# Attention followed by two MLPs: in five of the 24 head pairs both heads' values run on column halves, and the order of all instructions is planned anew

## The chip, the cores and the metric

The kernel runs on one core of one Trainium2 chip. Its engines are TensorE (PE in the profile, its weight loads PEld), VectorE (DVE), ScalarE (ACT), GpSimd (POOL) and SyncE (SP, which issues nearly all DMAs). The metric is the device time of one execution in microseconds (us); the lower, the better.

## The reference, cut to what matters

Three stages follow each other: an attention over 4 batches of 12 heads with 448 rows of 64, a first MLP with a softmax and a layer norm, and a second MLP with `h - tanh(h)`. All data are float32.

```python
def _attn_ref(q, k, v, g_q, g_k):
    q_n, k_n = (rmsnorm(q, g_q), rmsnorm(k, g_k))
    scores = scale * np.matmul(q_n, k_n.transpose(0, 1, 3, 2))
    scores = scores - np.max(scores, axis=-1, keepdims=True)
    attn = np.exp(scores)
    attn = attn / (np.sum(attn, axis=-1, keepdims=True) + 1e-09)
    return np.matmul(attn, v)
def _moe_ref(x, w_in, w_out, g_ln):
    h = x @ w_in
    e = np.exp(h - np.max(h, axis=-1, keepdims=True))
    solu = h * (e / (np.sum(e, axis=-1, keepdims=True) + 1e-09))
    ...
    return (ln @ w_out)
def _moe2_ref(x, w_in, w_out):
    h = x @ w_in
    return ((h - np.tanh(h)) @ w_out)
```

## The kernel before

The 48 heads are worked on as 24 pairs. For a pair, `qk_trans` transposes the normalised q and k (tile `qkps`), `maxima` forms the score rows to find their maxima (products `mps`, then a reduction `nm` on VectorE), `spread` brings the negated maxima into the operand of the next product (`nmps`, `nt`, and a DMA into `q`), and `weights` forms the transposed scores (`sps`) and their exponentials (`pf`, on ScalarE). `pv` multiplies them by the values. Its stationary operand is a tile `va` in which the 64 value columns of a chunk stand beside 64 columns of ones, so that one product gives 64 rows of sums weighted by the values and 64 rows of plain sums. It is a float32 product, and the profile has two records for each. A head has three chunks of 128 keys and a tail of 64; the tails of both heads lie on the two row halves of one tile, and `pv_tails` issues them one behind the other. So a pair has six full products and two tails, in two PSUM tiles `pvps`. `pv_fin` copies both halves of each out of PSUM on ScalarE (`sx`, `xu`), and `x_norm` divides and stores the result by a DMA (`xd`).

The first MLP runs in four blocks of tokens between the steps of the attention: its products are `hps` and `x2ps`, its transposes `lps`. Its weights are converted during the first blocks (tiles `raw`, `val`, `w`), saved to DRAM and loaded back later (`w<-w_in`, `w<-w_out`). The second MLP (`h2ps`, `ops`) follows when the attention is done.

Nothing of the order on the engines up to the end of the attention is the program's own: a `Recorder` takes each instruction down, and `place` plans a time for each from a table of costs. On each engine it takes the one with the lowest number in program order plus its entry in the table `SHIFT`. It adds margins for signals between engines (`slack`, two values: attention and MLP) and for DMAs (`doubt`), in us. Where the plan leaves TensorE without work, `fill` puts in products of a constant tile that nothing reads (tile `idle`, here called fillers). They stand in the program like any other product and run whether the wait for which they were planned comes or not.

```python
        took = 0.216 * (2 if since < self.warm else 1)
        n = int((start - since - 0.1) / took)
```

Since the recorder issues all instructions, they all carry the line L204.

Of the kernel before, what the change touches and what calls it, by code (L numbers as in the profile page):

```python
# [167 lines left out]
def _real(x):  # L168
# [3 lines left out]
SHIFT = {  # L172
    "bs vector": 61, "e scalar": 372, "gam scalar": 54, "gln scalar": -176, "glr load": -133, "grow load": 127,
    "hb scalar": 709, "hb vector": 727, "hps tensor": -61, "k scalar": 33, "k vector": -511, "lnT scalar": -27,
    "lnT vector": -468, "mv vector": -324, "nm vector": -5, "nmps tensor": -112, "nr scalar": 647, "nr vector": -428,
    "nt scalar": -1395, "ones vector": -357, "pf scalar": -1312, "pvps tensor": 76, "q gpsimd": -80, "q scalar": -59,
    "q sync": 43, "q vector": -148, "qd scalar": -121, "qd vector": 197, "qk load": 123, "qkps tensor": -1541,
    "qn gpsimd": -22, "qn vector": 18, "raw load": 176, "rr scalar": 128, "rr vector": 326, "rs gpsimd": 177,
    "rs vector": 7, "sm vector": 63, "sps tensor": 3, "sq scalar": 1359, "ss vector": 194, "sx scalar": -14,
    "va load": 108, "val scalar": 231, "val vector": -44, "w gpsimd": 21, "w scalar": -36, "w sync": 77,  # L180
    "w vector": -244, "w_in_ sync": -91, "w_out_ sync": 19, "wk scalar": 565, "wk vector": 5, "wq scalar": 1978,
    "x scalar": 22, "x2ps tensor": 312, "xd sync": 40, "xo scalar": 69, "xo vector": -253, "xr sync": -60,
    "xs scalar": 16, "xs vector": -126, "xu scalar": 232, "xu vector": 7, "zero vector": -3,
}


class Recorder:
# [14 lines left out]
    def take(self, eng, what, f, a, kw):  # L202
# [6 lines left out]
        outs = list(a[:1]) + [kw[n] for n in ("out", "accum_out") if n in kw]  # L209
        ins = list(a[1:]) + [x for n, x in kw.items() if n not in ("out", "accum_out")]  # L210
        op.out = outs[0]
# [25 lines left out]
        self.ops.append(op)  # L237

    def cost(self, op):
        n = 1  # L240
# [9 lines left out]
        if op.queue == "tensor":  # L250
            if op.what == "transpose":
                return (0.095 if n < 128 else 0.108), 0.2
            rhs = op.kw["rhs"]
            if rhs.root.dtype != F32:
                return 0.0025 + n * 0.000451, 0.2
            return (0.58 if rhs.p1 - rhs.p0 == 64 else 0.75), 0.2
# [48 lines left out]
    def transfer(self, op):  # L305
# [5 lines left out]
        return max(1, packets / 16.0) * (8 + 0.05 * run) * 1e-3  # L311

    def plan(self):
        for op in self.ops:
            op.after = 0.0
        for _ in range(self.passes):
            order = self.place()
            for op in self.ops:
                if op.eng == "dma" and not any(isinstance(x, View) for x in op.ins):
                    op.after = op.first - self.ahead  # L320
        return order

    def place(self):
# [36 lines left out]
        free = dict.fromkeys(("tensor", "vector", "scalar", "gpsimd", "sync"), 0.0)  # L360
        wire, lanes = 0.0, []
        ready = {e: [] for e in free}
        for op in ops:
# [29 lines left out]
        while placed < total:  # L393
# [28 lines left out]
            if e == "tensor" and start < self.warm:  # L422
                took *= 2
            if e == "vector" and op.what in ("tensor_tensor", "scalar_tensor_tensor", "tensor_scalar"):
                if took > 0.3 and not any(r.psum for r in op.refs) and start < free["gpsimd"]:
                    took += min(free["gpsimd"] - start, 1.1)
            if op.eng == "dma":
# [55 lines left out]
    warm = 9.0  # L483
    passes, ahead = 2, 185.2
    overlap = {"vector": 0.08, "scalar": 0.08, "gpsimd": 0.05}
    slack, doubt = (0.07, 0.18), 0.44
    still = None
# [11 lines left out]
def kernel(  # L499
# [180 lines left out]
    qk_t, qn_t, w_t, v_t, nm_t = {}, {}, {}, {}, {}  # L680
    pc_t, pv_t, xu_t, rb_t = {}, {}, {}, {}
    A = {}
    Q, K, qd = [], [], []

    def pair(p):
        return p // HP, 2 * (p % HP)
# [19 lines left out]
    def load_v(p):  # L706

        b, h = pair(p)
        t = v_t[p] = A["vh"].tile([128, 14, D], F32, tag="va", name="va")
        tv = t.rearrange("p (a z) d -> p a z d", z=2)  # L710
        nc.gpsimd.memset(tv[:, :, 1], 1.0)
        for i in range(2):
# [3 lines left out]
            )  # L716
        nc.sync.dma_start(out=tv[:, 6, 0], in_=v[b, h:h + 2, 384:448, :])

    def rsqrt(y, x, scale):
# [190 lines left out]
    def x_norm(p):  # L910
# [10 lines left out]
        nc.sync.dma_start(out=xd[:, hp, S * b:S * b + S], in_=xo)  # L921

    attn = []

    LAG = 7
# [4 lines left out]
    def step(i, *a):  # L930
        at(i // 4, i % 4, *a)

    for p in range(NP):
# [9 lines left out]
        for i in range(2):  # L943
            n, z = s + i, 4 * (s + i)
            for j, c in enumerate((3, 0, 1, 2) if i == 0 else (4, 5, 6)):
                step(z + j, maxima, p, c)
            step(z + 4, spread, n)
            for j in range(3):
                step(z + LAG + j, weights, n, j)
                step(z + LAG + 4 + j, pv, n, j)  # L950
        step(z + LAG + 3, weights, s + 1, 3)
        step(z + LAG + 4, pv_tails, s)
        step(z + LAG + 4, pv_fin, s)
        step(z + LAG + 6, pv_fin, s + 1)
        step(z + LAG + 8, x_norm, p)
    order = {maxima: 0, spread: 1, weights: 2, pv_tails: 3, pv: 4, pv_fin: 5}
    attn.sort(key=lambda e: (e[0], e[1], order.get(e[3], 6), e[2]))
# [421 lines left out]
```

## Time and profile before

| | us |
|---|---|
| median of 3 runs | 1060.19 |
| lowest and highest | 1055.9, 1064.42 |
| the profiled execution, its own time | 1062.6 |
| its span | 1060.8 |

The profiled execution has 1.8 us around its span and lies 2.4 us above the median. TensorE is busy through 98% of the span, and the attention ends at about 460 us. A time in the views counts from the start of the span.

### The profile page before, as it was taken

Reading aid. Unit: us, or ns where it says so; the run is one execution under the profiler, and the core shown is the slowest. Engines: PE = TensorE matmul, PEld = TensorE weight load, DVE = VectorE, ACT = ScalarE, POOL = GpSimd, SP = SyncE. Lnnn points to the kernel's source line nnn. Section 1 sums busy time; section 2 is a strip of 40 time slices with the busy share of each in tenths; the row PEclk is TensorE's granted clock in tenths of the full one; section 3 lists DMA queues with packets and bytes.
Section 4 is the critical chain, followed back from the end, with each engine's and each line's share of the span. In section 5 each row is a group of like instructions: output and inputs, shape, how many; then the busy total and the mean of one; then the engine's idle time right before and its main releaser. Section 6 shows DMA issues by size and latency. Waiting matters only on the chain.

```text
span 1060.8 us, 15538 instructions
## 1 busy us (share of the span) xinstructions
PE 1039.4 (98%) x5526; PEld 883.0 (83%) x5526; DVE 694.0 (65%) x1312; ACT 492.9 (46%) x996; POOL 235.1 (22%) x204
## 2 busy tenths in 40 slices
PE   8999999999999998999999999999999999999998
PEld 7666687677867887688999999898989999998987
DVE  8887877999898434557641373666767575765434
ACT  5888867888886544752451453212222221212110
POOL 3332223121122000025000251313333241422000
PEclk9999999999999998999999999999999999999999
DMA  7998999989999976387765421222212021110004
GB/s 188 212 255 239 245 259 275 256 219 303 300 311 332 266 205 188 112 274 249 253 229 189 164 62 59 60 61 60 60 40 78 22 61 43 57 60 1 1 30 179
DMA packets 112469, 171.20 MB, mean 161 GB/s; under 512 B 30656, under 2 KB 78216, under 8 KB 112392
## 3 DMA queue, kind: packets, MB, share of 16 engines
q1 hardware_dynamic: 112368, 170.20, 55.3%
q8 instruction: 44, 0.72, 0.3%
q14 instruction: 33, 0.27, 0.1%
q10 hardware_dynamic: 24, 0.01, 0.0%
HBM read 109.32 MB, written 29.10 MB: 130 GB/s over the span
## 4 chain that ended last, share of the span: by engine, by line
PE 87%; DMA 5%; DVE 4%; ACT 3%; issue 1%; SPq 0%; ACTq 0%; DVEq 0%
PE ops L204 22%; PE h2ps L204 22%; PE pvps L204 10%; PE hps L204 10%; PE x2ps L204 10%; PE sps L204 6%; PE mps L204 3%; PE qkps L204 2%; DMA raw<-in_moe_w_in_dram 1%; PE idle L204 1%; PE lps L204 1%; DVE nm L204 1%; ACT pf L204 1%; DMA w<-w_in 1%; DMA q<-nt 1%
## 5 line engine op out<-in xcount | busy, mean ns | idle before, releaser
L204 PE MATMUL ops<-w,gT 128*128 128x384 f32 x1344 | 257.5, 336 | 0.0
L204 PE MATMUL h2ps<-x2s,w 128*128 128x512 f32 (+1 forms) x1152 | 256.4, 365 | 0.0
L204 PEld LDWEIGHTS ops<-w,gT 128*128 128x128 f32 x1344 | 235.8, 188 | 8.4
L204 PEld LDWEIGHTS h2ps<-x2s,w 128*128 128x128 f32 x1152 | 200.2, 188 | 27.8
L204 DVE SCALAR_TENSOR_TENSOR val<-raw,val 128x512 int32<-128x512 int32 (+1 forms) x192 | 146.9, 767 | 63.4 <-POOL val L204 61.1
L204 DVE TENSOR_TENSOR ob<-ops,ob 128x384 f32<-128x384 f32 x196 | 108.3, 553 | 102.4 <-PE ops L204 102.0
L204 POOL TENSOR_TENSOR w<-val,w 128x512 fp32r<-128x512 f32 x60 | 80.7, 1347 | 380.5 <-ACT w L204 380.5
L204 PE MATMUL pvps<-pf,va 128*128 128x448 f32 (+1 forms) x384 | 158.5, 555 | 0.0
L204 PE MATMUL hps<-w,xs 128*128 128x256 f32 (+1 forms) x828 | 133.6, 315 | 3.2 <-DMA w<-w_in 3.2
L204 DVE TENSOR_REDUCE nm<-mps 128x1 f32<-128x448 f32 x168 | 101.0, 617 | 54.2 <-PE mps L204 53.3
L204 PE MATMUL sps<-q,k 128*128 128x448 f32 (+2 forms) x400 | 130.0, 430 | 6.1 <-ACT pf L204 3.1
L204 PEld LDWEIGHTS hps<-w,xs 128*128 128x128 f32 x828 | 118.8, 195 | 15.8 <-issue 3.5
L204 PE MATMUL x2ps<-lnT,w 128*128 128x384 f32 (+1 forms) x720 | 125.1, 328 | 0.3 <-DVE lnT L204 0.3
L204 PEld LDWEIGHTS x2ps<-lnT,w 128*128 128x128 f32 x720 | 118.2, 189 | 3.0 <-issue 1.5
L204 ACT ACTIVATE th<-h2ps 128x512 f32<-128x512 f32 (+1 forms) x64 | 34.8, 544 | 179.9 <-PE h2ps L204 161.9
L204 PEld LDWEIGHTS sps<-q,k 128*128 128x128 f32 (+2 forms) x400 | 68.9, 182 | 44.3 <-issue 18.6
L204 ACT ACTIVATE pf<-sps 128x448 f32<-128x448 f32 (+1 forms) x169 | 87.9, 537 | 31.0 <-PE sps L204 28.7
L204 PEld LDWEIGHTS pvps<-pf,va 128*128 128x128 f32 (+1 forms) x384 | 61.1, 188 | 37.5 <-issue 33.9
L204 POOL TENSOR_SCALAR val<-raw 128x512 f32<-128x512 f32 x48 | 80.1, 1670 | 25.1 <-DMA raw<-in_moe_w_out_dram 11.9
L204 ACT ACTIVATE gT<-th 128x512 fp32r<-128x512 f32 (+1 forms) x64 | 37.1, 579 | 98.6 <-PE ops L204 66.8
L204 POOL TENSOR_TENSOR qn<-qk,rr 112x512 f32<-112x512 f32 x44 | 50.2, 1159 | 118.2 <-DVE rr L204 60.8
L204 DVE TENSOR_TENSOR th<-h2ps,th 128x512 f32<-128x512 f32 (+1 forms) x64 | 39.7, 621 | 44.2 <-ACT th L204 44.1
(95 smaller groups left out, 992.1 us busy)
## 6 DMA issues: line engine op xcount, KB each, us to landing
w<-w_out SPq DMA_DIRECT2D x48, 512.0 KB
raw<-in_moe_w_in_dram SPq DMA_DIRECT2D x36, 512.0 KB
raw<-in_moe_w_out_dram SPq DMA_DIRECT2D x36, 512.0 KB
w<-w_in SPq DMA_DIRECT2D x24, 512.0 KB
q<-wq SPq DMA_DIRECT2D x46, 224.0 KB
k<-wk SPq DMA_DIRECT2D x46, 224.0 KB
w_in<-w SPq DMA_DIRECT2D x12, 512.0 KB
w_out<-w SPq DMA_DIRECT2D x12, 512.0 KB
```

Source lines behind the costliest of these rows:

```text
L204: return f(*[_real(x) for x in a], **{n: _real(x) for n, x in kw.items()})
```

## The change

For pairs 16 to 20 (`halves = range(16, 21)`) the products with the values are written differently. `load_v2` loads the values alone, without columns of ones and without GpSimd's memset. `pv2` issues for each chunk the products of both heads one behind the other: each has 64 columns, head 0 writes partitions 0 to 63 of one PSUM tile and head 1 partitions 64 to 127. `sums` adds the four exponential tiles of a head on GpSimd (three adds a head, of which the tails have 64 partitions), and `pv_sums` multiplies both heads' added tiles by 64 columns of ones on the two halves (`sups`). `x_norm2` works straight from the two PSUM tiles instead of `pv_fin`'s copies: two ScalarE instructions and three on VectorE a pair, where before there were six and three. The planner counts such a pair of products as one instruction of 0.76 us.

In the program this takes 40 products `pvps` of 128 columns away, and brings 40 of 64 columns and 10 `sups`; 30 adds come to GpSimd and 5 memsets go; 20 ScalarE instructions go. Of the rest only one kind of instruction has another count: the fillers are 162 instead of 88.

The planner has another rule for VectorE and GpSimd instructions that use SBUF at the same time, other margins (`slack`, `doubt`, `ahead`), and another `SHIFT`.

```diff
@@ -170,17 +170,19 @@
 SHIFT = {
-    "bs vector": 61, "e scalar": 372, "gam scalar": 54, "gln scalar": -176, "glr load": -133, "grow load": 127,
...
+    "bs vector": 1852, "e scalar": -388, "gam scalar": 178, "gln scalar": -555, "glr load": 501, "gps tensor": 103,
...
 }
@@ -207,7 +209,9 @@
         op.queue, op.what, op.f, op.a, op.kw = eng, what, f, a, kw
         op.at, op.rank = len(self.ops), self.rank
         outs = list(a[:1]) + [kw[n] for n in ("out", "accum_out") if n in kw]
-        ins = list(a[1:]) + [x for n, x in kw.items() if n not in ("out", "accum_out")]
+        ins = list(a[1:]) + [x for n, x in kw.items() if n not in ("out", "accum_out", "ins")]
+        for one in kw.get("ins", ()):
+            ins += [one["lhsT"], one["rhs"]]
         op.out = outs[0]
         name = op.out.root.args[3].rstrip("0123456789") if isinstance(op.out, View) else "-"
         load = op.eng == "dma" and not any(isinstance(x, View) for x in a[1:] + tuple(kw[n] for n in kw if n != "out"))
@@ -236,6 +240,14 @@
                 root.log = keep
         self.ops.append(op)
 
+    def both(self, two):
+        def f(**kw):
+            for one in two:
+                self.tensor.real.matmul(**{n: _real(x) for n, x in one.items()})
+
+        a, b = two
+        self.take("tensor", "both", f, (), dict(out=a["out"], accum_out=b["out"], ins=[a, b]))
+
     def cost(self, op):
         n = 1
         for d in (op.out.shape if isinstance(op.out, View) else [1, 1])[1:]:
@@ -250,6 +262,8 @@
         if op.queue == "tensor":
             if op.what == "transpose":
                 return (0.095 if n < 128 else 0.108), 0.2
+            if op.what == "both":
+                return 0.76, 0.2
             rhs = op.kw["rhs"]
             if rhs.root.dtype != F32:
                 return 0.0025 + n * 0.000451, 0.2
@@ -309,6 +323,13 @@
         if run < 64:
             return 0.025 * packets
         return max(1, packets / 16.0) * (8 + 0.05 * run) * 1e-3
+
+    @staticmethod
+    def shares(op):
+        if op.queue == "gpsimd":
+            return op.what != "memset"
+        two = op.what in ("tensor_tensor", "scalar_tensor_tensor", "tensor_scalar")
+        return op.queue == "vector" and two and not any(r.psum for r in op.refs)
 
     def plan(self):
         for op in self.ops:
@@ -359,6 +380,7 @@
         opened = dict.fromkeys(queue, 0)
         free = dict.fromkeys(("tensor", "vector", "scalar", "gpsimd", "sync"), 0.0)
         wire, lanes = 0.0, []
+        lock = {"vector": 0.0, "gpsimd": 0.0}
         ready = {e: [] for e in free}
         for op in ops:
             if op.left == 0:
@@ -421,9 +443,10 @@
             took, late = self.cost(op)
             if e == "tensor" and start < self.warm:
                 took *= 2
-            if e == "vector" and op.what in ("tensor_tensor", "scalar_tensor_tensor", "tensor_scalar"):
-                if took > 0.3 and not any(r.psum for r in op.refs) and start < free["gpsimd"]:
-                    took += min(free["gpsimd"] - start, 1.1)
+            if op.eng != "dma" and self.shares(op):
+                other = lock["gpsimd" if e == "vector" else "vector"]
+                took += max(other - start, 0.0)
+                lock[e] = start + took
             if op.eng == "dma":
                 if len(lanes) >= 8:
                     start = max(start, lanes[-8])
@@ -481,9 +504,9 @@
     notice = {"tensor": 0.02, "gpsimd": 0.045}
     lag = 0
     warm = 9.0
-    passes, ahead = 2, 185.2
+    passes, ahead = 2, 202.6
     overlap = {"vector": 0.08, "scalar": 0.08, "gpsimd": 0.05}
-    slack, doubt = (0.07, 0.18), 0.44
+    slack, doubt = (0.12, 0.39), 0.94
     still = None
 
     def give(self):
@@ -678,7 +701,8 @@
 
 
     qk_t, qn_t, w_t, v_t, nm_t = {}, {}, {}, {}, {}
-    pc_t, pv_t, xu_t, rb_t = {}, {}, {}, {}
+    pc_t, pv_t, xu_t, rb_t, su_t = {}, {}, {}, {}, {}
+    halves = range(16, 21)
     A = {}
     Q, K, qd = [], [], []
 
@@ -704,6 +728,10 @@
 
 
     def load_v(p):
+
+        if p in halves:
+            load_v2(p)
+            return
 
         b, h = pair(p)
         t = v_t[p] = A["vh"].tile([128, 14, D], F32, tag="va", name="va")
@@ -715,6 +743,16 @@
                 in_=v[b, h + i, 0:384, :].rearrange("(c p) d -> p c d", p=128),
             )
         nc.sync.dma_start(out=tv[:, 6, 0], in_=v[b, h:h + 2, 384:448, :])
+
+    def load_v2(p):
+
+        b, h = pair(p)
+        t = v_t[p] = A["vh"].tile([128, 14, D], F32, tag="va", name="va")
+        for i in range(2):
+            nc.sync.dma_start(
+                out=t[:, 3 * i:3 * i + 3], in_=v[b, h + i, 0:384, :].rearrange("(c p) d -> p c d", p=128)
+            )
+        nc.sync.dma_start(out=t[:, 6], in_=v[b, h:h + 2, 384:448, :])
 
     def rsqrt(y, x, scale):
 
@@ -920,6 +958,57 @@
         nc.vector.scalar_tensor_tensor(out=xo, in0=sx, scalar=-2.0, in1=xu, op0=ALU.add, op1=ALU.mult)
         nc.sync.dma_start(out=xd[:, hp, S * b:S * b + S], in_=xo)
 
+    def pv2(p, j):
+
+        if j == 0:
+            pv_t[p, 2] = ps_v.tile([128, 4, CP], F32, tag="v", name="pvps")
+        ps = pv_t[p, 2]
+        two = []
+        for i in range(2):
+            r = slice(64 * i, 64 * i + 64)
+            k = r if j == 3 else slice(0, 128)
+            two.append(dict(
+                out=ps[r], lhsT=v_t[p][k, 6 if j == 3 else 3 * i + j], rhs=pc_t[2 * p + i, j][k],
+                start=j == 0, stop=j == 3,
+            ))
+        nc.both(two)
+
+    def sums(n, j):
+
+        p, i = divmod(n, 2)
+        if i == 0 and j == 1:
+            rb_t[p] = A["one"].tile([128, S], F32, tag="sx", name="sx")
+            xu_t[p] = A["xu"].tile([128, S], F32, tag="xu", name="xu")
+        r = slice(64 * i, 64 * i + 64) if j == 3 else slice(0, 128)
+        o = (rb_t, xu_t)[i][p][r]
+        x, y = (pc_t[n, jj][r].rearrange("r c q -> r (c q)") for jj in (0, j))
+        nc.gpsimd.tensor_tensor(out=o, in0=x if j == 1 else o, in1=y, op=ALU.add)
+
+    def pv_sums(p):
+
+        ps = su_t[p] = ps_m.tile([128, 4, CP], F32, tag="m", name="sups")
+        nc.both([
+            dict(
+                out=ps[64 * i:64 * i + 64].rearrange("r c q -> r (c q)"), lhsT=nc.still[:, 0:64],
+                rhs=(rb_t, xu_t)[i][p], start=True, stop=True,
+            )
+            for i in range(2)
+        ])
+
+    def x_norm2(p):
+        b, hp = divmod(p, HP)
+        su, xu = (t.rearrange("r c p -> r p c") for t in (su_t.pop(p), pv_t.pop((p, 2))))
+        xo = A["xo"].tile([128, S], F32, tag="xo", name="xo")
+        y, t = rb_t.pop(p), xu_t.pop(p)
+        xo4, y4, t4 = (z.rearrange("r (p c) -> r p c", c=4) for z in (xo, y, t))
+
+        nc.scalar.activation(out=y4, in_=su, func=AF.Ln, bias=tiny)
+        nc.scalar.activation(out=y, in_=y, func=AF.Exp, scale=-1.0)
+        nc.vector.scalar_tensor_tensor(out=t4, in0=su, scalar=tiny, in1=y4, op0=ALU.add, op1=ALU.mult)
+        nc.vector.scalar_tensor_tensor(out=xo4, in0=xu, scalar=-1.0, in1=y4, op0=ALU.mult, op1=ALU.mult)
+        nc.vector.scalar_tensor_tensor(out=xo, in0=t, scalar=-2.0, in1=xo, op0=ALU.add, op1=ALU.mult)
+        nc.sync.dma_start(out=xd[:, hp, S * b:S * b + S], in_=xo)
+
     attn = []
 
     LAG = 7
@@ -945,15 +1034,30 @@
             for j, c in enumerate((3, 0, 1, 2) if i == 0 else (4, 5, 6)):
                 step(z + j, maxima, p, c)
             step(z + 4, spread, n)
+            if p in halves:
+                for j in range(3):
+                    step(4 * s + LAG + 2 * j + i, weights, n, j)
+                    if j:
+                        step(4 * s + LAG + 2 * j + i + 1, sums, n, j)
+                for j in (0, 1) if i == 0 else (2, 3):
+                    step(4 * s + LAG + 2 * j + 2, pv2, p, j)
+                continue
             for j in range(3):
                 step(z + LAG + j, weights, n, j)
                 step(z + LAG + 4 + j, pv, n, j)
+        if p in halves:
+            step(4 * s + LAG + 6, weights, s + 1, 3)
+            step(4 * s + LAG + 7, sums, s, 3)
+            step(4 * s + LAG + 7, sums, s + 1, 3)
+            step(4 * s + LAG + 9, pv_sums, p)
+            step(4 * s + LAG + 10, x_norm2, p)
+            continue
         step(z + LAG + 3, weights, s + 1, 3)
         step(z + LAG + 4, pv_tails, s)
         step(z + LAG + 4, pv_fin, s)
         step(z + LAG + 6, pv_fin, s + 1)
         step(z + LAG + 8, x_norm, p)
-    order = {maxima: 0, spread: 1, weights: 2, pv_tails: 3, pv: 4, pv_fin: 5}
+    order = {maxima: 0, spread: 1, weights: 2, pv_tails: 3, pv: 4, pv_fin: 5, sums: 3, pv_sums: 4, pv2: 5}
     attn.sort(key=lambda e: (e[0], e[1], order.get(e[3], 6), e[2]))
     attn_i = [0]
 
```

The first place is TensorE at the products with the values of pair 16. `mps` and `nmps` are of the next pair, `sps` the scores of pair 17. Before:

```order
L204 MATMUL pvps<-pf,va 128x448 x2
L204 MATMUL mps<-k_178,q_161 128x448
L204 MATMUL pvps<-pf,va 128x448
L204 MATMUL mps<-k_178,q_161 128x448 x2
L204 MATMUL sps<-q_180,k_170 128x448 x2
L204 MATMUL pvps<-pf,va 128x448 x2
L204 MATMUL sps<-q_180,k_170 128x448 x4
L204 MATMUL nmps<-idf,nm 4x128
L204 MATMUL pvps<-pf,va 128x448
L204 MATMUL mps<-k_178,q_161 128x448
L204 MATMUL pvps<-pf,va 128x448 x2
```

After the change, the same place:

```order
L246 MATMUL pvps<-pf,va 64x448 x6
L206 MATMUL sps<-q_187,k_175 128x448 x2
L206 MATMUL nmps<-idf,nm 4x128
L206 MATMUL mps<-k_182,q_167 128x448 x2
L246 MATMUL pvps<-pf,va 64x448 x2
L206 MATMUL mps<-k_182,q_167 128x448
L206 MATMUL idle<-still 128x128
L206 MATMUL mps<-k_182,q_167 128x448
L206 MATMUL idle<-still 128x128
L206 MATMUL mps<-k_182,q_167 128x448
L206 MATMUL idle<-still 128x128
L206 MATMUL mps<-k_182,q_167 128x448
```

The eight products of 128 columns, which stood between others, are eight of 64 columns, six of them in a row, and single fillers stand between the `mps` that follow.

The second place is TensorE at the first products `x2ps` of the MLP's first block, a little later. Before:

```order
L204 MATMUL pvps<-pf,va 128x448 x2
L204 MATMUL mps<-k_178,q_161 128x448 x2
L204 MATMUL x2ps<-lnT,w_3794 128x384 x3
L204 MATMUL mps<-wk,qd_183 128x448
L204 MATMUL x2ps<-lnT,w_3794 128x384 x6
L204 MATMUL nmps<-idf,nm 4x128
L204 MATMUL x2ps<-lnT,w_3794 128x384 x3
L204 MATMUL x2ps<-lnT,w_3800 128x384 x3
L204 MATMUL sps<-q_180,k_170 128x448 x6
L204 MATMUL x2ps<-lnT,w_3800 128x384
L204 MATMUL sps<-q_180,k_170 128x448 x2
L204 MATMUL sps<-q_180,k_170 64x448 x2
```

After the change, at the same first two weight tiles of `x2ps`:

```order
L246 MATMUL pvps<-pf,va 64x448 x2
L246 MATMUL sups<-sx,still 64x448
L246 MATMUL sups<-xu,still 64x448
L246 MATMUL pvps<-pf,va 64x448 x2
L206 MATMUL idle<-still 128x128 x16
L206 MATMUL x2ps<-lnT,w_4034 128x384 x12
L206 MATMUL x2ps<-lnT,w_4055 128x384 x12
L206 MATMUL idle<-still 128x128 x12
L206 MATMUL sps<-q_167,k_182 128x448 x2
L206 MATMUL idle<-still 128x128 x3
L206 MATMUL sps<-q_167,k_182 128x448 x4
L206 MATMUL idle<-still 128x128 x2
```

The attention's products stood between the `x2ps`; now these are two runs of 12, with 16 fillers ahead and 12 behind. Counted over the program, 45 fillers stood ahead of the first `sps` and now 61; from the `mps` before the first column half to pair 18's values there are 68 where 13 stood in the corresponding stretch; elsewhere 33 for 30.

The third place is GpSimd about pairs 16 and 17. `rs` belongs to the layer norm, `qn` to the normalising of q and k. Before:

```order
L204 TENSOR_TENSOR rs<-rs,mhalf 128x1
L204 MEMSET va 128x7x64
L204 TENSOR_TENSOR rs<-rs,mhalf 128x1
L204 MEMSET va 128x7x64
L204 TENSOR_TENSOR qn<-qk,rr 112x2x4x64
L204 TENSOR_TENSOR rs<-rs,mhalf 128x1
L204 TENSOR_TENSOR qn<-qk,rr 112x2x4x64 x5
L204 MEMSET va 128x7x64
L204 TENSOR_TENSOR qn<-qk,rr 112x2x4x64 x2
L204 MEMSET va 128x7x64 x3
L204 TENSOR_TENSOR qn<-qk,rr 112x2x4x64 x2
```

After the change:

```order
L206 TENSOR_TENSOR sx<-pf 128x448
L206 TENSOR_TENSOR xu<-pf 128x448
L206 TENSOR_TENSOR sx<-sx,pf 128x448
L206 TENSOR_TENSOR xu<-xu,pf 128x448
L206 TENSOR_TENSOR sx<-sx,pf 64x448
L206 TENSOR_TENSOR xu<-xu,pf 64x448
L206 TENSOR_TENSOR sx<-pf 128x448
L206 TENSOR_TENSOR sx<-sx,pf 128x448
L206 TENSOR_TENSOR xu<-pf 128x448
L206 TENSOR_TENSOR sx<-sx,pf 64x448
L206 TENSOR_TENSOR xu<-xu,pf 128x448
L206 TENSOR_TENSOR xu<-xu,pf 64x448
```

Two pairs' adds stand one behind the other, twelve in a row, where before memsets and `qn` stood.

## Rows read from the trace of the kernel before

**Rows 1.** page, part 1: busy time, share of the span, instructions

```profile
PE 1039.4 (98%) x5526; PEld 883.0 (83%) x5526; DVE 694.0 (65%) x1312; ACT 492.9 (46%) x996; POOL 235.1 (22%) x204
```

**Rows 2.** six stretches: us, busy us of each engine, granted clock, DMA share, GB/s

```profile
0.00:23.00 23.00, 19.18 (x117) 16.75 (x118) 19.95 (x57) 12.14 (x30) 5.81 (x15) 0.93 0.77 190
23.00:150.00 127.00, 124.29 (x584) 84.93 (x583) 100.64 (x192) 102.20 (x217) 38.99 (x40) 1.00 0.93 237
150.00:300.00 150.00, 148.53 (x804) 109.95 (x802) 131.59 (x278) 123.11 (x277) 26.22 (x30) 1.00 0.96 275
300.00:330.00 30.00, 27.11 (x126) 21.14 (x125) 29.90 (x71) 24.69 (x53) 9.01 (x8) 0.94 1.04 303
330.00:460.00 130.00, 124.90 (x661) 99.94 (x660) 60.75 (x118) 71.15 (x142) 10.47 (x13) 0.97 0.73 212
460.00:600.00 140.00, 139.15 (x816) 129.27 (x815) 65.51 (x127) 49.48 (x85) 26.50 (x21) 1.00 0.70 229
```

**Rows 3.** waits of PE: releaser, us in total, times, longest

```profile
PE hps L204 <- DMA w<-w_in: 3.2, 1, 3.2
PE sps L204 <- ACT pf L204: 3.1, 2, 1.7
PE sps L204 <- DVE nm L204: 2.1, 2, 1.8
PE qkps L204 <- POOL qn L204: 1.1, 1, 1.1
```

**Rows 4.** timeline of PE behind its two longest waits: start, us, instruction, [wait]

```profile
323.95 0.68 PE L204 MATMUL sps<-q,k 128*128 128x448 f32 x2 [1.80 <-DVE nm L204]
...
407.66 1.44 PE L204 MATMUL hps<-w,xs 128*128 128x256 f32 x5 [3.23 <-DMA w<-w_in]
```

**Rows 5.** stretches behind those two waits, columns as in Rows 2

```profile
324.00:330.00 6.00, 6.00 (x25) 5.65 (x26) 6.00 (x20) 4.68 (x8) 2.07 (x2) 0.72 1.07 256
404.00:414.00 10.00, 6.77 (x34) 6.50 (x33) 0.19 (x1) 0.87 (x3) 0.00 (x0) 0.66 0.49 169
```

**Rows 6.** timeline: full PV products, two tails together, one tail alone, next rows

```profile
313.06 0.19 PEld L204 LDWEIGHTS pvps<-pf,va 128*128 128x128 f32 x1 [0.18 <-issue]
...
313.43 0.19 PEld L204 LDWEIGHTS pvps<-pf,va 128*128 128x128 f32 x1 [0.18 <-issue]
...
129.62 1.02 PE L204 MATMUL pvps<-pf,va 64*128 64x448 f32 x4
130.57 0.47 PE L204 MATMUL sps<-q,k 128*128 128x448 f32 x1
...
54.23 1.02 PE L204 MATMUL pvps<-pf,va 64*128 64x448 f32 x2
55.18 0.47 PE L204 MATMUL mps<-k,q 128*128 128x448 f32 x1
```

**Rows 7.** timeline of PE: eight fillers in a row

```profile
320.21 1.95 PE L204 MATMUL idle<-still 128*128 128x128 f32 x16
```

**Rows 8.** timeline of POOL and DVE: the same operations together and alone

```profile
309.35 3.44 POOL L204 TENSOR_TENSOR qn<-qk,rr 112x512 f32<-112x512 f32 x2 [5.00 <-DMA q<-nt]
...
311.41 1.99 DVE L204 TENSOR_SCALAR val<-val 128x512 f32<-128x512 f32 x1
...
313.92 0.40 DVE L204 TENSOR_SCALAR val<-val 128x512 int32<-128x512 int32 x1
...
331.92 2.05 POOL L204 TENSOR_TENSOR qn<-qk,rr 112x512 f32<-112x512 f32 x2 [5.11 <-issue]
```

**Rows 9.** groups of ACT that read pvps: busy us, mean ns

```profile
L204 ACT ACTIVATE sx<-pvps,tiny 64x448 f32<-64x448 f32 x48 | 30.2, 629 | 16.7 <-PE pvps L204 15.9
...
L204 ACT ACTIVATE xu<-pvps 64x448 f32<-64x448 f32 x48 | 25.7, 536 | 0.8
```

More of the change, by code (lines that the diff above doesn't have):

```diff
@@ L172 @@
 SHIFT = {
-    "bs vector": 61, "e scalar": 372, "gam scalar": 54, "gln scalar": -176, "glr load": -133, "grow load": 127,
[L174 to L182, printed above, removed]
@@ L183 @@
-    "xs scalar": 16, "xs vector": -126, "xu scalar": 232, "xu vector": 7, "zero vector": -3,
+    "bs vector": 1852, "e scalar": -388, "gam scalar": 178, "gln scalar": -555, "glr load": 501, "gps tensor": 103,
+    "grow load": 1261, "grow vector": 4, "hb scalar": 144, "hb vector": -38, "k scalar": 965, "k sync": -12,
+    "k vector": -1076, "lnT scalar": -431, "lnT vector": 102, "lps tensor": 20, "mps tensor": -13, "mv vector": 115,
+    "nm vector": 64, "nmps tensor": -404, "nr scalar": 103, "nr vector": 15, "nt scalar": -256, "ones vector": 833,
@@ new lines @@
+    "pf scalar": -486, "pvps tensor": 173, "q gpsimd": 473, "q scalar": -930, "q sync": -21, "q vector": -615,
+    "qd scalar": -315, "qd vector": -561, "qk load": 16, "qkps tensor": 4, "qn gpsimd": 773, "qn vector": 916,
+    "raw load": 101, "rr scalar": 119, "rr vector": 572, "rs gpsimd": -491, "rs vector": -919, "sm vector": 388,
+    "sps tensor": -41, "sq scalar": -272, "ss vector": -132, "sups tensor": 23, "sx gpsimd": -720, "sx scalar": -94,
+    "sx vector": 84, "va gpsimd": 327, "va load": -29, "val scalar": -324, "val vector": 469, "w gpsimd": 73,
@@ L184 @@
+    "w scalar": 242, "w sync": 503, "w vector": -165, "w_in_ sync": -241, "w_out_ sync": -138, "wk scalar": -111,
+    "wk vector": 30, "wq scalar": -83, "wq vector": -156, "x scalar": -136, "x2d sync": -279, "x2ps tensor": 297,
+    "xd sync": -16, "xo scalar": -451, "xo vector": -838, "xr sync": -63, "xs scalar": -335, "xs vector": 281,
+    "xu gpsimd": -528, "xu scalar": -40, "xu vector": 63, "zero vector": -257,
 }
```

## The prediction

> **What bounds the kernel now.** I read the page first: TensorE is busy through 98% of the span, VectorE 65%, ScalarE 46%, GpSimd 22% [rows 1]. So time can only be won by taking work or waits from TensorE, or lost by giving it either. The stretches show where that is possible [rows 2]. After 460 us TensorE idles for 0.9 us in 140, and the change leaves that part's instructions alone; up to 460 us it idles for 3.8 us in the first 23, then 2.7, 1.5, 2.9 and 5.1, which is 12.2 us from 23 to 460. From 300 to 330 us VectorE has no room: 29.9 us busy of 30, while TensorE has 27.1. From 330 on it is the other way round: TensorE 124.9 of 130, VectorE 60.8. Pair 16's values are computed at about 300 us, pair 17's at 316, pair 18's at 340, pair 20's at 400. So the change lies with two pairs in a stretch that VectorE bounds, and with three in one that TensorE bounds.
>
> The list of waits names what ended the idle time: a weight tile's DMA 3.2 us, exponentials 3.1, maxima 2.1, the normalised q and k 1.1 [rows 3]. Two waits are long, 1.80 and 3.23 us [rows 4], and what follows them is dear too: in the 6 us behind the first the mean granted clock is 0.72, in the 10 us around the second 0.66 [rows 5], a mixture of full speed and the half level of 1.2 GHz. That costs 0.28 x 6 + 0.34 x 10 = 5.1 us of work, beside the waits themselves.
>
> **The change part by part.** The sum is made against the profiled execution (1062.6 us, with 1.8 us around its span). It lies 2.4 us above the median of 1060.2, so I add the difference to the median.
>
> *Products with the values, before.* The two passes of a full product follow each other by 0.37 us, seen at their weight loads, so a product is about 0.75. Two tails together run from 129.62 to 130.57, which is 0.95 us, and a tail alone from 54.23 to 55.18, as much: the second tail of a pair is free, but a pass on half an array costs 0.48 instead of 0.37 [rows 6]. A pair is 6 x 0.75 + 0.95 = 5.45 us.
>
> *After.* Five pairs of half products for each pair of heads (four with values, one with ones). No row shows column halves. The nearest shows row halves, and by it they run side by side in 0.95 us: 4.75 us a pair, 0.70 saved. If they ran side by side in the time of a full product, it would be 3.75, and 1.70 saved. If one ran behind the other as full products, 7.5, and 2.05 lost. I take 0.70, since the row has the same operands' size and type and two tiles in the array. The Trainium skill (TensorEngine Tiling, Key Properties) says that tiles work independently and in parallel, and that a change of the tiling mode drains the engine. The first sentence without the second would give the 1.70 (8.5 us in all); the tail alone, at 0.95 against 0.75, bears out that half tiles are not had at the full product's price.
>
> Of the five pairs' 3.5 us, the 1.4 of pairs 16 and 17 lie where TensorE waits for VectorE, and I count them as nothing there. That leaves **-2.1 us** (bounds -8.5 and +10.3, all five pairs at either end).
>
> *Fillers.* Eight of them (16 records) take 1.95 us, with the last one's end in it, so 0.22 us each [rows 7]. The order has 162 instead of 88, and TensorE executes them in turn, wait or no wait: 74 x 0.22 = **+16.3 us**, 3.5 of them before the first `sps`, 12.1 about pairs 16 to 18, 0.7 elsewhere. This is the one term that is certain.
>
> *Waits.* What speaks for the fillers is that they stand where waits would have been, and that they hold the clock up. At most they and the larger margins take all waits from 23 to 460 us (12.2), the loss of clock (5.1), and 2.8 of the 3.8 at the start, whose first microsecond waits for the constant tile itself: 20.1 us. At least nothing. A plan with larger margins puts each product later in the order than its operands, and the short waits should go; but no plan knows when the 3.2 us DMA lands. I take 60%, **-12 us**.
>
> *The other engines.* ScalarE loses two `sx` of 0.63 and two `xu` of 0.54 us a pair, 11.7 us in all [rows 9]; it is busy for 71 of 130 us in the stretch where that matters, so it gives nothing back. VectorE has three instructions a pair as before. GpSimd gets 30 adds. Its nearest row is `qn`, 2.05 us for two when nothing disturbs them [rows 8], so about 1.03 each or 6.2 a pair. GpSimd has 10.5 us of work in 130, and can hold that. Its adds are in the way of VectorE, though, and that is a rival below. In the forecast I count them as covered by the fillers that the plan put into just this stretch; if that cover fails, the rival's price falls due. The SP queue has the same instructions in another order; what is moved past the weight loads there is within the bounds of the waits.
>
> Sum: 16.3 - 2.1 - 12 = +2.2 us. Profiled that would be 1064.8, against the median **1062.4**, so I say 1062.
>
> **Rivals.**
>
> *The waits go, the halves are cheap.* The same terms at their good ends: 16.3 - 8.5 - 20.1 = -12.3 us, 1048. For it: two waits with their loss of clock make 10.1 us of the 20.1, and neither needs to be in the new order. Against: 68 fillers stand where 13 stood, so the plan itself has found nothing to put there. Chance 0.15, of which 0.11 below 1% faster.
>
> *The adds hold VectorE up.* While GpSimd worked on `qn`, a `tensor_scalar` on VectorE took 1.99 us where its like took 0.40 right after, and the two `qn` took 3.44 instead of 2.05 [rows 8]. So an instruction of VectorE that meets one of GpSimd waits it out. Pairs 16 and 17 bring twelve adds, one behind the other, into the stretch in which VectorE is full. If each holds up one instruction for its own 1.03 us, VectorE ends there 12.4 us later; the maxima come behind the conversions in its queue, `nt` and `sps` behind the maxima, and TensorE with them. It decides as soon as the conversions of the weights last until pair 17, as they did before (to 331 us). Of the fillers' wait a part is meant for this; beyond it I price it at 10 us, and 1.7 for the clock behind one more long wait: 1074. The Trainium skill (GPSIMD Engine Reference, Key points) says that GpSimd shares its SBUF interfaces with VectorE, with contention for instructions with two SBUF inputs or in a 2-port mode; the pair of rows agrees. It speaks against putting adds beside conversions. Chance 0.14. This is the case on the slow side.
>
> *The halves don't run side by side*, so the change does not do what it says: +10.3 instead of -2.1 on TensorE gives 16.3 + 10.3 - 12 = +14.6, 1075. Against it: the row halves do. For it: two column halves each stream all 128 partitions, which two row halves don't. Chance 0.09.
>
> **How the numbers follow.** The forecast has 0.62. Its own range, by waits of -4 to -18, is 1056 to 1070. The range of 1048 to 1075 takes in the good ends of all terms and both slow rivals at their prices. What a measurement of this kernel can tell from no change is about 1%, or 10.6 us. Faster than that: 0.11 from the first rival, 0.01 else. Slower: 0.09 and 0.07 from the two slow rivals, and 0.03 from a forecast whose waits stay. The rest, 0.69, is within 1%.
>
> **What would show it.** In the profile after, the group `idle` should have 324 records and some 40 us. The four passes of two half products should be done in about 0.95 us; 0.75 would be the good end, 1.5 the bad one. The waits of TensorE between 23 and 460 us should have shrunk to some 6 us, and the clock should be 0.98 or more in all stretches. If a `val` or `w` on VectorE takes 1.4 us or more in numbers between 290 and 340 us, and `sps` waits for `nm`, the second rival is at work. The stretch after the attention should have the same length to a microsecond. The forecast is wrong if the waits grow although fillers stand before them, or if the end of the attention moves by over 10 us.

## The result, and the profile after

The changed kernel takes 1073.5 us (median; 1071.3 to 1074.4) where the kernel before takes 1059.6: a ratio of 1.0125, interval 1.008 to 1.017. Run again beside other kernels it gave 1.0108 (1.005 to 1.017). The profiled execution has a span of 1072.2 us; before it was 1060.8. So it is slower by a little over 1%. That is 11.5 us above the forecast of 1062, and within the range near its slow end of 1075.

I read the profile after in the order of the prediction. First the busy time from the page's part 1, which answers to [rows 1]:

```profile
PE 1048.7 (98%) x5694; PEld 886.8 (83%) x5694; DVE 701.2 (65%) x1312; ACT 479.2 (45%) x976; POOL 269.5 (25%) x229
```

TensorE has 9.3 us more work, ScalarE 13.7 less, GpSimd 34.4 more. The fillers alone are 45.7 us instead of 27.3, so TensorE's own work, without them, is 9.1 us less. The same six stretches as in [rows 2] (us; busy us of PE, PEld, DVE, ACT, POOL; granted clock; DMA share; GB/s):

```profile
0.00:23.00 23.00, 20.76 (x141) 18.30 (x142) 20.39 (x60) 12.96 (x31) 6.26 (x16) 1.00 0.86 210
23.00:150.00 127.00, 123.41 (x597) 83.79 (x596) 97.55 (x192) 96.91 (x215) 39.99 (x40) 1.00 0.90 237
150.00:300.00 150.00, 147.48 (x789) 107.00 (x787) 126.86 (x260) 120.29 (x268) 35.02 (x34) 1.00 0.92 249
300.00:330.00 30.00, 30.00 (x211) 25.37 (x210) 27.74 (x49) 19.46 (x47) 7.21 (x6) 1.00 1.05 316
330.00:460.00 130.00, 122.47 (x698) 97.01 (x697) 73.82 (x150) 64.97 (x132) 37.47 (x35) 0.97 0.74 226
460.00:600.00 140.00, 135.82 (x769) 123.12 (x769) 66.12 (x127) 51.64 (x88) 22.90 (x19) 0.99 0.69 223
```

The idle time of TensorE from 23 to 460 us is 3.6 + 2.5 + 0 + 7.5 = 13.6 us, against 12.2 before; from 460 to 600 us it is 4.2 against 0.9, and in the first 23 us 2.2 against 3.8. Between 300 and 330 us TensorE has no idle time left, but this is filler: the stretch 300 to 350 us holds 13.7 us of fillers (1.95 before) and 6.7 us of idle time (3.0 before). Together that is 20.4 us of fillers and idle time, against 4.9 before.

The waits of TensorE, as in [rows 3] (releaser, us in total, times, longest):

```profile
PE nmps L206 <- DVE nm L206: 6.4, 1, 6.4
PE mps L206 <- ACT pf L206: 3.9, 5, 1.2
PE hps L206 <- ACT hb L206: 3.3, 1, 3.3
```

The two long waits of before [rows 4] are gone, and two others stand here. The first, on the timeline of PE (start, us, instruction, wait):

```profile
334.64 0.47 PE L206 MATMUL mps<-k,q 128*128 128x448 f32 x1 [0.20 <-ACT pf L206]
341.54 0.37 PE L206 MATMUL nmps<-idf,nm 128*4 128x128 f32 x1 [6.43 <-DVE nm L206]
```

What `nm` stood behind is read on VectorE's timeline, and what that waited for on GpSimd's:

```profile
330.96 0.62 DVE L206 SCALAR_TENSOR_TENSOR xo<-xu,xo 128x448 f32<-128x448 f32 x1
337.42 1.61 DVE L206 SCALAR_TENSOR_TENSOR val<-raw,val 128x512 f32<-128x512 f32 x1 [5.83 <-POOL val L206]
338.95 2.00 DVE L206 SCALAR_TENSOR_TENSOR w<-val,gln,w 128x128 fp32r<-128x128 f32 x4
340.87 0.61 DVE L206 TENSOR_REDUCE nm<-mps 128x1 f32<-128x448 f32 x1
```
```profile
335.87 1.51 POOL L206 TENSOR_SCALAR val<-raw 128x512 f32<-128x512 f32 x1 [21.75 <-DMA raw<-in_moe_w_in_dram]
337.35 1.13 POOL L206 TENSOR_TENSOR sx<-pf 128x448 f32<-128x448 f32 x1
```

Read backwards: TensorE waits for pair 19's maxima, with the last of pair 18's scores (`sps`) behind them in its queue; the maxima stand in VectorE's queue behind a `val` of the second MLP's first weight tile; that waits for GpSimd's `val`, and this for the tile's load, which SP issued at 329.74 us. The issue in the kernel after, and under it the same loads in the kernel before, whose first stands at 306.6 us:

```profile
329.74 2.14 SPq L206 DMA_DIRECT2D raw<-in_moe_w_in_dram  x1
```
```profile
L204 SPq DMA_DIRECT2D raw<-in_moe_w_in_dram x3: 368/406/472, 306.6 to 325.3; - x3
```

VectorE idles for 5.8 us with ready work behind the blocked instruction, four `w` and `nm`. The tile is first used by `h2ps`, at 554 us. The granted clock behind this wait (stretch, us, PE busy, clock, DMA):

```profile
338.00:342.00 4.00, 0.46 (x2) 0.70 0.92 352
342.00:346.00 4.00, 4.00 (x13) 0.50 0.65 238
346.00:350.00 4.00, 4.00 (x20) 0.95 0.47 138
```

Four microseconds at the level of 1.2 GHz after 6.4 idle ones: about 2 us more. The second wait, 3.34 us before `hps` at 506.39, has the same form on ScalarE:

```profile
498.57 0.63 ACT L206 ACTIVATE w<-val 128x512 fp32r<-128x512 f32 x1 [4.09 <-DVE val L206]
505.22 0.63 ACT L206 ACTIVATE w<-val 128x512 fp32r<-128x512 f32 x1 [6.02 <-DVE val L206]
505.76 1.07 ACT L206 ACTIVATE hb<-hps 128x512 f32<-128x512 f32 x2
```

The copy `w` of another tile of the second MLP waits for its conversion, and `hb`, which frees TensorE's PSUM buffers, stands behind it. From 507 to 510 us the clock is 0.50 again:

```profile
507.00:510.00 3.00, 3.00 (x8) 0.50 0.98 319
```

In the profile of the second measurement of this kernel the first wait is there as before (6.7 us), but the waits for `hb` are only 1.8 us, in two pieces.

The column halves do what they should. Three pairs of half products in a row, and the row after them, on PE's timeline; and a pair with ones by itself:

```profile
287.79 2.48 PE L246 MATMUL pvps<-pf,va 128*64 128x448 f32 x12
290.19 0.47 PE L206 MATMUL sps<-q,k 128*128 128x448 f32 x1
...
299.34 0.59 PE L246 MATMUL sups<-sx,still 128*64 128x448 f32 x1
299.34 0.59 PE L246 MATMUL sups<-xu,still 128*64 128x448 f32 x1
299.76 0.54 PE L246 MATMUL sups<-sx,still 128*64 128x448 f32 x1
299.77 0.54 PE L246 MATMUL sups<-xu,still 128*64 128x448 f32 x1
300.24 1.48 PE L206 MATMUL sps<-q,k 128*128 128x448 f32 x6
```

The two halves start together, and three pairs take 2.40 us up to the next row, 0.80 each; one alone takes 0.90.

### The profile page after: what moved, and what is told of

The parts are those of the page before. It is cut to its first block, busy times and chain, and to the rows that moved or that the text cites. A ratio compares the mean times of both kernels' runs of the same rounds, so it can differ in the third digit from the quotient of the medians.

```text
span 1072.2 us, 15875 instructions
## 1 busy us (share of the span) xinstructions
PE 1048.7 (98%) x5694; PEld 886.8 (83%) x5694; DVE 701.2 (65%) x1312; ACT 479.2 (45%) x976; POOL 269.5 (25%) x229
## 4 chain that ended last, share of the span: by engine, by line
PE 82%; DMA 6%; ACT 4%; DVE 4%; issue 1%; SPq 1%; POOL 0%; ACTq 0%; DVEq 0%; POOLq 0%
PE ops L206 22%; PE h2ps L206 22%; PE hps L206 9%; PE x2ps L206 9%; PE pvps L206 7%; PE sps L206 5%; PE mps L206 3%; DMA xd<-xo 1%; PE idle L206 1%; PE qkps L206 1%; DMA raw<-in_moe_w_in_dram 1%; SPq L206 1%; PE pvps L246 1%; DMA q<-wq 1%; DMA raw<-in_moe_w_out_dram 1%
## 5 line engine op out<-in xcount | busy, mean ns | idle before, releaser
L206 DVE SCALAR_TENSOR_TENSOR val<-raw,val 128x512 int32<-128x512 int32 (+1 forms) x192 | 151.1, 790 | 64.1 <-POOL val L206 61.7
L206 PE MATMUL hps<-w,xs 128*128 128x256 f32 (+1 forms) x828 | 129.6, 313 | 3.3 <-ACT hb L206 3.3
L206 PEld LDWEIGHTS hps<-w,xs 128*128 128x128 f32 x828 | 116.3, 192 | 14.7 <-ACT hb L206 3.8
L206 PE MATMUL sps<-q,k 128*128 128x448 f32 (+2 forms) x400 | 125.4, 430 | 2.5 <-ACT pf L206 1.3
L206 PE MATMUL pvps<-pf,va 128*128 128x448 f32 (+1 forms) x304 | 123.6, 555 | 0.0
L206 PE MATMUL x2ps<-lnT,w 128*128 128x384 f32 (+1 forms) x720 | 121.6, 326 | 0.3 <-DVE lnT L206 0.3
L206 PEld LDWEIGHTS pvps<-pf,va 128*128 128x128 f32 (+1 forms) x304 | 47.6, 188 | 27.6 <-issue 24.3
```

Of the source, the lines that this page charges most:

```text
L206: return f(*[_real(x) for x in a], **{n: _real(x) for n, x in kw.items()})
```

## The experiments

**Theories.** M: the loss is in two waits, in which conversions for the second MLP stand ahead of the attention's work in an in-order queue, with the clock lost behind them, and in the fillers. A: the half products and GpSimd's adds carry it (rival 2 of the prediction, in its wide form). B: the new order is slower throughout.

**The late tile.** In the changed kernel's `fetch`, two loads wait for pair 18's output:

```diff
+                if kind == "in2" and i < 2:
+                    nc.sync.dma_start(out=t[0:1, 0, 0, 0:1], in_=xd[0:1, 0, 1344:1345].bitcast(I32))
                 nc.sync.dma_start(out=t, in_=src)
```

> The changed kernel, all of it, with one thing moved: the first two weight tiles of the second MLP are loaded and converted only after pair 18's output is stored (about 360 us instead of 330). Theory M (the loss comes from 18 us of fillers and from two new waits in the queues of VectorE and ScalarE, 6.4 and 3.3 us long with a half clock behind them, against which the half products win 8 us): the wait of nmps for nm at 341 us goes, and the half clock behind it, 6.4 + 3.4 us, so 1062 to 1067. Rival A (half products and GpSimd's adds themselves carry the loss, the conversions only stand where it shows): the same maxima come late by the adds, and the time stays at 1071 to 1075. Rival B (the order planned anew is slower throughout): no change beyond 3 us.

Measured: 1066.4 us, ratio 1.0017 (0.999 to 1.0045). The wait at 341 us is gone. The stretches 300 to 330 and 330 to 460 us:

```profile
300.00:330.00 30.00, 30.00 (x208) 24.77 (x207) 27.00 (x49) 21.09 (x52) 7.27 (x6) 1.00 1.04 297
330.00:460.00 130.00, 127.50 (x733) 100.37 (x731) 75.41 (x157) 67.23 (x138) 37.20 (x35) 1.00 0.79 244
```

All adds, halves and fillers are still there, and the clock is 1.00. From 300 to 350 us fillers and idle time are 14.1 + 0.1 = 14.2 us instead of 20.4. Most of the loss goes with the place of two conversions; A and B both said that it wouldn't.

**And ScalarE's queue freed.** On top of that, the first six rounded copies go to VectorE:

```diff
-                nc.scalar.activation(out=w[:, 0], in_=x, func=AF.Copy)
+                if not save and self.nc < 6:
+                    nc.vector.tensor_copy(out=w[:, 0], in_=x)
+                else:
+                    nc.scalar.activation(out=w[:, 0], in_=x, func=AF.Copy)
```

> As the kernel with the second MLP's first tiles late, and the rounded copies of its first six weight tiles are made by VectorE, so that no copy that waits for a conversion stands ahead of hb in ScalarE's queue. Theory M (two waits in in-order queues carry the loss): the wait of hps for hb near 500 us (2.3 us there, 3.3 in the changed kernel) goes, with the half clock behind it, 3 to 4 us less: 1061 to 1064, level with the kernel before. Against M: VectorE's six copies come late themselves and the wait moves to another place, 1066.

Measured: 1064.05 us where the kernel before had 1062.2 among the same runs, ratio 1.0008 (0.9988 to 1.0027); the profiled span is 1060.7, as before. ScalarE now has the five `hb` in one piece, right behind the product that they wait for:

```profile
493.53 3.33 ACT L206 ACTIVATE hb<-hps 128x512 f32<-128x512 f32 x5 [6.99 <-PE hps L206]
```

With both queues freed, the changed kernel is level with the one before, and it does not beat it. That the wait for `hb` cost time isn't shown by this: 1.0008 and the 1.0017 of the late tile alone lie within each other's intervals.

**Without fillers.** Three kernels, by the same edit: the changed one, the one before, and the one with the late tile.

```diff
-        if n < 1 or not keys:
+        if start > 30.0 or n < 1 or not keys:
```

> The changed kernel in the same order without the 101 fillers that its plan puts after 30 us. If fillers add their full time, 101 x 0.23 = 23 us less: 1050. If they fill waits and hold the clock up, no change: 1070 to 1076, with as many microseconds of waits as fillers went, or more. Theory M takes a part: the fillers about pairs 16 to 18 stand where TensorE waits anyway in this order, so 5 to 12 us less, 1061 to 1069. Rivals A and B say nothing on it.

> The kernel before in its own order, without the 40 fillers that its plan puts after 30 us. If a filler costs its full time, 40 x 0.23 = 9 us less: about 9 us below the kernel before. If fillers only stand in time in which TensorE would wait or fall to half clock, no change within 3 us, and the waits of TensorE up to 460 us grow by as much as the fillers took; so it was in the changed kernel, where 101 fewer fillers moved the time by nothing, and so I expect it here.

> The changed kernel with the second MLP's first tiles late (as in the run that moved them behind pair 18) and without the 101 fillers after 30 us. If fillers cost their time once the long wait of VectorE's queue is gone, up to 101 x 0.16 = 16 us less than with them: 1050 to 1058. If they only stand in waits, as they did in the changed kernel and in the one before, no change: 1063 to 1068, and the waits of TensorE up to 460 us grow by 10 us or more.

Measured: 1073.4 us, ratio 1.0097 (1.006 to 1.0135; the changed kernel 1.0125 and 1.0108); 1059.9 (the kernel before 1060.35 beside it, ratio 0.9985, 0.995 to 1.002); 1067.1, ratio 1.0039 (1.0017 to 1.006), no better than 1.0017 with fillers. In none can a cost of the fillers behind 30 us be told from nothing (those ahead of it were kept). M had expected 5 to 12 us from the first of the three, and missed: the fillers are no part of the loss. The changed kernel without fillers, and under it the kernel before without them, from 300 us:

```profile
300.00:330.00 30.00, 22.31 (x118) 16.69 (x116) 25.66 (x43) 18.39 (x45) 7.04 (x6) 0.87 1.04 303
330.00:460.00 130.00, 121.82 (x675) 94.10 (x674) 72.54 (x148) 64.08 (x129) 36.93 (x35) 0.95 0.72 222
```
```profile
300.00:330.00 30.00, 25.78 (x111) 19.03 (x111) 28.50 (x66) 24.13 (x53) 9.19 (x8) 0.94 1.03 304
330.00:460.00 130.00, 123.83 (x661) 98.78 (x661) 62.17 (x126) 72.06 (x143) 10.47 (x13) 0.99 0.77 215
```

Here the order itself shows. From 23 to 460 us the new order waits 27.2 us and the old one 19.7, and the new one's clock is lower too. The fillers cover half of the new order's waits and hold its clock up.

**One part without the other.** The new table, margins and cost rule with no pair on halves (`halves = range(0)`); and the halves with the old table, margins and rule.

> The new table, margins and cost rule with no pair on column halves (all pairs as in the kernel before); 136 fillers. Theory M: 48 fillers more than before make 11 us, nothing is won on the products, and waits stay about as they were: 1068 to 1080. Rival A (halves and adds carry the loss): 1058 to 1064, like the kernel before. Rival B: as slow as the changed kernel or slower, 1072 to 1085, with its long waits there too.

> Half products and GpSimd's adds of pairs 16 to 20 as in the changed kernel, but planned with the table, margins and cost rule of the kernel before; 123 fillers. Theory M: 35 fillers more than before at 0.23 us make 8, the half products take 8 off, and a table that was not made for this work adds some waits: 1057 to 1068. Rival A (the halves and adds themselves carry the loss): 1070 or more, with waits of sps or nmps around 290 to 350 us. Rival B (the new table and margins carry it): like the kernel before or faster, 1050 to 1061.

Measured: 1068.3 us, ratio 1.0058 (1.0036 to 1.0079); and 1065.3, ratio 1.0007 (0.9984 to 1.0029). So the halves are not what loses, which is against A. Set beside the late tile's 1.0017, which has the same plan with halves and no long wait either, they win 0.4%; by the medians, 1068.3 and 1066.4, it is 1.9 us, or 0.2%, and the two intervals overlap a little. Under the old plan they win nothing that can be told. The new plan alone costs 0.6%, at the lower edge of what M expected (1068 to 1080); M took that from its fillers, and by the three kernels above they are hardly the reason. Which of its waits make the 0.6% was not separated.

**The halves twice.** Each pair of half products is issued twice and accumulated, so values and sums both double:

```diff
-            for one in two:
-                self.tensor.real.matmul(**{n: _real(x) for n, x in one.items()})
+            for again in range(2):
+                for one in two:
+                    one = {n: _real(x) for n, x in one.items()}
+                    one["start"], one["stop"] = one["start"] and not again, one["stop"] and bool(again)
+                    self.tensor.real.matmul(**one)
```

> The changed kernel with each pair of half products issued twice, accumulated in the same tile (values and sums both double, so their ratio stays): 25 more pairs of products and sums. If two halves run side by side at a full product's pace (0.75 us, 0.90 with entry and exit) and TensorE is the bound there, 25 x 0.75 = 19 us more, 1088 to 1094. If they ran one behind the other, 37 us more, 1108 or above. If TensorE waits in the stretch anyway and the repeats fill waits or take the place of what fillers cover, less: 1078 to 1086.

Measured: 1087.4 us, 14.75 above the changed kernel's 1072.65 beside it, or 0.59 us for each of 25 pairs. Halves one behind the other are out. Of the 4 us by which it falls short of 25 x 0.75, the long wait took 2.2: it is 4.5 us here instead of 6.7. The rest was not traced.

**Short adds.**

```diff
+        if j > 1:
+            o, y = o[:, 0:8], y[:, 0:8]
         nc.gpsimd.tensor_tensor(out=o, in0=x if j == 1 else o, in1=y, op=ALU.add)
```

> The changed kernel in the same order, in which the second and third adds of each head cover 8 of 448 columns, so most of the sums of the exponentials of the later chunks are left out; GpSimd has 20 adds less, nearly 20 us of its work. Rival A (GpSimd's adds hold VectorE up, and that is what the change loses): the conversions on VectorE at 337 to 348 us take 0.69 instead of 1.6, the wait of nmps at 341 us shrinks by more than half, 1064 to 1068. Theory M (the wait comes from a late load and from where its conversions stand in VectorE's queue, and the adds only lengthen it): the wait loses at most 1 to 2 us of its 6.4, 1069 to 1073.

Measured: 1072.5 us, ratio 1.0104, as slow as the changed kernel. It isn't the clean test that its text promises: the plan prices an add by its size, so the order came out another, and no wait of TensorE at 341 us is over 1 us in it. What it does show is the adds' effect on VectorE. The group `val<-raw,val` from 334 to 350 us (ns min/median/max), in the changed kernel and under it with short adds:

```profile
L206 DVE SCALAR_TENSOR_TENSOR val<-raw,val x5: 693/1577/1619, 337.4 to 349.3; 128x512 int32<-128x512 int32 x3, 128x512 f32<-128x512 f32 x2
```
```profile
L206 DVE SCALAR_TENSOR_TENSOR val<-raw,val x6: 673/680/693, 340.6 to 349.1; 128x512 int32<-128x512 int32 x4, 128x512 f32<-128x512 f32 x2
```

An add makes a conversion 0.9 us longer; taking 20 adds nearly away gives no time back. The Trainium skill (GPSIMD Engine Reference, Key points) says that GpSimd and VectorE share their SBUF interfaces; these two rows agree with it.

This kernel also bears on theory M. It has no long wait of TensorE and a clock of 1.00 from start to end, and yet it is as slow. The late tile is late in it too, and holds VectorE up for 4 us:

```profile
340.64 1.30 DVE L206 SCALAR_TENSOR_TENSOR val<-raw,val 128x512 f32<-128x512 f32 x2 [4.05 <-POOL val L206]
```

From 300 to 350 us it has 16.2 us of fillers and 3.2 of idle time, together 19.4, near the 20.4 of the changed kernel and 5 more than with the late tile moved. So the loss needs no long wait of TensorE; fillers can stand in its place. By the ratios 1.0104 and 1.0017 it is 9 us, and where the other 4 go was not found; nor was the tile moved in this kernel.

**Fewer and other pairs under the old plan.** Pairs 18 to 20, and 18 to 23 (`halves = range(18, 21)` and `range(18, 24)` in the kernel with the old plan).

> The order planned as in the kernel before, and only pairs 18 to 20 on column halves, which lie behind the stretch that VectorE bounds (300 to 330 us); pairs 16 and 17 stay whole. If what the five-pair version under the old plan lost lies with pairs 16 and 17 in that stretch, 4 to 7 us less than it: 1055 to 1060 where the kernel before has 1060. If the halves win nothing anywhere, or a change of the order alone costs some us, the same as before or up to 5 us more.

> The same with pairs 18 to 23 on column halves. If each pair behind 330 us wins the 1 to 1.5 us that TensorE is spared, 3 to 4 us less than with three pairs: 1051 to 1057. If the attention's end is set by the chain from exponentials to the sums on GpSimd and not by TensorE's time, no gain on the three: 1055 to 1062, with waits of sups for sx at 440 to 460 us.

Both missed: 1072.0 us, ratio 1.009 (1.0065 to 1.0115), and 1071.4, ratio 1.0086 (1.0055 to 1.0116). I had looked for the loss in pairs 16 and 17, and without their halves the time was longer, not shorter (1.0007 with them, under the same plan). With three pairs the wait is 5.0 us before `sps` at 333.83, on `nm`, and on VectorE and GpSimd stands:

```profile
329.31 0.69 DVE L204 SCALAR_TENSOR_TENSOR val<-raw,val 128x512 f32<-128x512 f32 x1 [4.81 <-POOL val L204]
...
333.17 0.60 DVE L204 TENSOR_REDUCE nm<-mps 128x1 f32<-128x448 f32 x1
```
```profile
327.75 1.52 POOL L204 TENSOR_SCALAR val<-raw 128x512 f32<-128x512 f32 x1 [7.07 <-DMA raw<-in_moe_w_in_dram]
```

It is the chain of the changed kernel, in another plan, with no add near it and `val` at 0.69 us. The kernel with six pairs has the same wait, of 6.4 us. So the adds aren't needed for the wait; a late load and a conversion in front of `nm` are enough. That it is what makes these two kernels slow isn't shown: moving the tile in them wasn't tried.

## Why the prediction was right or wrong

The range held, but by luck: its slow end was the price of rivals whose mechanisms did not come, or only in part. The likeliest case, within 1% of the kernel before (0.69), did not come; the measured ratio is 1.0125. Two of its three terms were wrong, and the third too small. By the prediction's own signs it was wrong as well: the idle time from 23 to 460 us grew to 13.6 us where some 6 were asked, although fillers stand before it, and the last product with the values starts at 470.0 us where it started at 456.9, over 10 us later.

- **Fillers, "the one term that is certain", +16.3 us: this is the step that failed.** Their number came as said (324 records), and their busy time is 45.7 us, 18.4 more than before. But TensorE's time in a filler isn't time lost: 101, 40 and 101 fewer took nothing off in three kernels. I priced an instruction by its duration on an engine that executes in order, and did not ask whether that engine had anything else to do there. In the stretch 300 to 350 us it had not. The same mistake stands at the prediction's start, where a busy share of 98% is read as TensorE bounding the kernel: fillers are part of that share, and TensorE's own work fell by 9.1 us while the span grew by 11.4.
- **Waits, -12 us: failed too.** From 23 to 460 us the idle time came to 1.4 us more and behind that, up to 600, to 3.3 more; only the first 23 us gave 1.6 back. The two waits that I meant to see vanish did, and the clock in the first 23 us rose from 0.93 to 1.00. The term rested on the margins of the plan, and the plan doesn't hold all of the work: the recorded order ends before the second MLP's tiles are asked for (`rec.give()` comes ahead of `w2`), and their loads and conversions are put between the planned instructions afterwards. No margin guards against those. I said that SP's instructions moved past the weight loads lie within the bounds of the waits, and never looked at where the first of these tiles stood: issued at 306.6 us before, at 329.74 after.
- **Products with the values, -2.1 us: right in mechanism, undersized on TensorE.** By row halves I took 0.95 us for a pair of half products; it is 0.80 in a group of three and 0.90 alone. Of the 25 pairs 9 stand in three groups and 16 alone, so they take about 21.6 us where the products before took 5 x 5.45 = 27.25: 5.6 us less. In time they gave back less than that, 1.9 us at the new plan by medians and nothing at the old one. The halves work side by side, and a group costs 0.15 us beyond its passes (2.40 against 3 x 0.75, and 0.90 against 0.75). The Trainium skill (TensorEngine Tiling, Key Properties) says that tiles work in parallel and that a change of the mode drains the engine; the trace shows the first, and the 0.15 us fits the second, though no run separates what it is made of.
- **ScalarE gives nothing back: right**, it lost 13.7 us of work and no time came of it.
- **Rival 2 (1074) came nearest in time, with half of its mechanism.** The maxima do come late behind conversions, `nt` and `sps` behind them. But what holds the conversions up is a late load (5.8 of the 6.4 us), not the adds, which lengthen one `val` and one `w` in the chain by 0.9 us each; and it isn't at pairs 16 and 17 but at pair 18's scores and pair 19's maxima. Rival 3 is out, and rival 1 had nearly the right price of the halves with the wrong fate of the waits.
- **The stretch after the attention: right.** From the first `h2ps` to the end of the span it is 518.9 us before and 517.8 after.

Put together by ratios: 1.0125 (or 1.0108) as changed; 1.0017 with the late tile out of VectorE's queue; 1.0008 with ScalarE's queue freed too. The place of the late tile carries most of the loss, shown by moving it; the share of ScalarE's queue is below what these runs can tell. What is left near zero is the new plan's own cost, 0.6%, whose cause stays open, against the halves' gain of 0.2 to 0.4%.

## What to carry to other kernels

A filler's price is what its removal gives back, not its duration; read it as a mark of where the order has nothing to do, and count idle and filler time together. Where a planner orders a part of a program, look for what is put into its queues afterwards: one conversion whose load comes late blocks everything behind it, and it is moved for little by making its load depend on something later. When a change plans an order anew, compare the plan alone with the change alone before judging either; here a gain of a few tenths of a per cent lay under a loss of 1%, most of it by one blocked queue.

## What the runs showed of the hardware

Two column halves of fp32 products, 128 by 64 on 448 columns, run at the pace of one full product (0.80 us a pair in a group), where two row halves took 0.95 us. An add of GpSimd on 64 partitions is as dear as one on 128: the group `sx<-sx,pf` has five of each between 1.12 and 1.42 us.
